# One slot moved in the matrix engine's accumulators: three buffers for a layer's sums, one for the transposes

## The chip, the core and the metric

The kernel runs on one core of a Trainium2 chip. A core has a matrix engine (PE), which writes its sums into a small memory of eight banks, PSUM; a vector engine (DVE) and a scalar engine (ACT), which read PSUM and write SBUF, the working memory; a general engine (POOL); and queues (SP among them) that issue transfers (DMA). Every engine runs its own instructions in order and waits for others by semaphores. The metric is the device time of one execution in microseconds (us), the median of several runs.

## What is computed

The reference runs a recurrence over 768 steps (its result, after a transposition, is x with 3072 tokens of 320 values), then two feed-forward networks. The first is a mixture of experts: each token goes to the expert with the largest logit. The second takes every token.

```python
def _moe_ref(x, modality_id, w_gate, modality_bias, w1, w2):
    logits = x @ w_gate + modality_bias[modality_id]
    e_idx = np.argmax(logits, axis=1)
    ...
    for e in range(E):
        mask = e_idx == e
        ...
        h = np.maximum(x[mask] @ w1[e], 0.0)
        out[mask] = gate_w[mask, None] * (h @ w2[e])

def _moe2_ref(x, w_gate, w_val, w_out):
    g = x @ w_gate
    silu = g * (1.0 / (1.0 + np.exp(-g)))
    val = x @ w_val
    return (silu * val @ w_out).astype(np.float32)
```

Here D is 320, there are 8 experts with 1024 hidden values, and the second network has 1536.

## The kernel before

The recurrence and the routing take the first part of the execution and are not touched. The change lies in `Moe.main`, which does both networks and begins at about 568 us.

*Numbers in two halves.* Each operand of a product is kept as a rounded part and the rest (xh and xl, h and l, hh and hl), and a product is three matmuls into the same sums (`mm3`, L685 to L687). For the last 64 of the 320 input values, both halves share one tile, so there are two matmuls (L695, L696). One *up-projection* (`up`, here called an up) is 8 matmuls: 128 hidden values for all tokens of a group, 384 or 512 columns wide, into one tile `pu`. One *down-projection* (`down`) is 9 or 12 matmuls of 320 columns into the tiles `pd`, one for each 128 tokens, which gather the sums over all hidden values.

*First network.* Tokens sorted by expert come in 8 groups (`sj`), the second of them with 512 tokens, the others with 384. Each group takes 4 passes (`c`), each with two ups; the first group does one up at a time. A pass consists of two ups, their emptying (`evac`: ACT's Relu into hh at L1007, then DVE's hl at L1008), and the two down-projections of the pass before, with splits of the next weights (L745, L746), pieces of the conversion of the second network's weights (`prepare`, which calls L644 to L653) and one token tile of the next group between them. The string `ORD` sets their order. Such a token tile (`xtile`) is three transposes on PE (L729) into one tile `xt`, and its split (`xsplit`): ACT's two copies at L699, then DVE's xl (L700) and x (L701). The first three passes of a group have one each, the fourth has none. Only the second group is made ready in one go: its tile 0 in the last pass of the first group, then, at L1112 to L1117, tiles 1, 2 and 3 with one down-projection behind tile 1.

*A loop for what is left* (L1080 to L1096) stands between, for tokens that eight groups don't hold. With these inputs it runs no times; its branch is a meeting point of all engines.

*Second network.* Tokens come in blocks of 256 or 384, with 12 steps over the hidden values; blocks 0 to 3 do 6 steps each in a first round and 6 in a second one. A step takes two ups (`pg`, `pv`), ACT's Silu of the one (L1192), DVE's product with the other (L1194), ACT's hh (L1197), DVE's hl (L1201) and the down-projections of the step before. Token tiles of the next block (`xt2`, after ACT's product with the gate at L1060) come one in a step, on three following steps. Up to about 850 us the weights are still being converted.

*PSUM.* Three pools share the eight banks, and a tile fills one:

```python
psX=ctx.enter_context(tc.tile_pool(name="psX",bufs=2,space=PS))
psU=ctx.enter_context(tc.tile_pool(name="psU",bufs=2,space=PS))
psD=ctx.enter_context(tc.tile_pool(name="psD",bufs=4,space=PS))
px=lambda: psX.tile([128,3,128],F32,tag="xt",name="xt")
def put(n): return psU.tile([128,WIDE],F32,tag="pu",name="pu")[:,0:n]
```

A pool gives its buffers in turn, and the first write into a buffer waits until everything that read its last tile has ended. The first pool also serves the routing's few products (`rt`), and `put` serves both networks' ups.

Of the kernel before, what the change touches and what calls it, by code (L numbers as in the profile page):

```python
# [15 lines left out]
PS = bass.MemoryType.PSUM  # L16
# [552 lines left out]
SL=384; WIDE=512; NSTAT=8; NMAX=16; NT=SL//128; ROWS=NMAX*SL+WIDE-SL  # L569
# [5 lines left out]
def first(j):  # L575

    return NT*j+((WIDE-SL)//128 if j>1 else 0)
# [110 lines left out]
def up(T,out,w,x,fs,between=None):  # L688


    wh,wl=w; xh,xl,x2=x
    for k in range(2):
        mm3(T,out,wh[:,k,fs],wl[:,k,fs],xh[:,k],xl[:,k],k==0,False)
        if between and k==0: between()
    T.matmul(out,wh[:,2,fs],x2,start=False,stop=False)  # L695
    T.matmul(out,wl[:,2,fs],x2,start=False,stop=True)  # L696
# [5 lines left out]
class Moe:  # L702
# [266 lines left out]
    def main(s, LG, y1, gd, wg, wv, wo, out):  # L969
        tc=s.tc; nc=s.nc; V,A,G,T=nc.vector,nc.scalar,nc.gpsimd,nc.tensor; C=s.C  # L970
        s.gd=gd
        with ExitStack() as ctx:
# [1 line left out]
            s.stp=ctx.enter_context(tc.tile_pool(name="stp",bufs=2))  # L974
            W,between,nbetween=moe2_weights(tc,pool,s.stp,wg,wv,wo)
            P=ctx.enter_context(tc.tile_pool(name="m1",bufs=1)); s.wp.append(P)
            psX=ctx.enter_context(tc.tile_pool(name="psX",bufs=2,space=PS))
            psU=ctx.enter_context(tc.tile_pool(name="psU",bufs=2,space=PS))
            psD=ctx.enter_context(tc.tile_pool(name="psD",bufs=4,space=PS))
            px=lambda: psX.tile([128,3,128],F32,tag="xt",name="xt")  # L980
            def put(n): return psU.tile([128,WIDE],F32,tag="pu",name="pu")[:,0:n]
# [23 lines left out]
            def evac(pu,n):  # L1005
                hh,hl=hht(n)
                A.activation(hh,pu,AF.Relu)  # L1007
                V.scalar_tensor_tensor(hl,pu,0.0,hh.bitcast(F32),ALU.max,ALU.subtract)  # L1008
                return hh,hl
            def down(pd,first,last,hh,hl,wh,wl):  # L1010
                for i in range(len(pd)):
                    ts=slice(128*i,128*i+128)
                    mm3(T,pd[i][:,0:320],hh[:,ts],hl[:,ts],wh,wl,first,last)
            def ystile(): return P.tile([128,WIDE//128,322],F32,tag="ys",name="ys")
            def store(pd,rows,ids,last=False):
                ys=ystile()[:,0:len(pd)]
                V.tensor_copy(ys[:,:,320:322].bitcast(I32),ids)
                for i in range(len(pd)):
                    (V.tensor_copy if i in (0,3) else A.copy)(ys[:,i,0:320],pd[i][:,0:320])
                    if last: nc.sync.dma_start(rows[128*i:128*i+128],ys[:,i])  # L1020
                if not last: nc.sync.dma_start(rows.rearrange("(i p) d -> p i d",p=128),ys)
# [52 lines left out]
            def loop(n):  # L1074

                wx=W["g"]; ws=W["v"]
                f=lambda t: t.bitcast(F32)
                x=(wx[0][:,0:2,512:896],wx[1][:,0:2,512:896],wx[0][:,2,512:896]); h1=tuple(t[:,:,896:1024] for t in wx)
                h2=tuple(t[:,0:1,896:1216] for t in ws); hh=tuple(t[:,2,896:1280] for t in ws)
                with tc.If(n>NSTAT), tc.For_i(NSTAT,n,1) as jr:  # L1080
                    xg=[s.xg() for i in range(NT)]
                    s1=s.stp.tile([128,3,128],F32,tag="cvm",bufs=1,name="s1r"); s2=s.stp.tile([128,1,320],F32,tag="cva",bufs=1,name="s2r")
                    ix=P.tile([128,NT,2],I32,tag="id",bufs=6,name="id")
                    V.tensor_copy(ix[:],R['slot'][:,bass.ds(jr*NT+(first(2)-3*NT),NT)])
                    e=nc.sync.value_load(R['ei'][0:1,bass.ds(jr,1)],min_val=0,max_val=7)
                    for i in range(NT):
                        G.indirect_dma_start(xg[i][:,0:320],None,s.xd,IOA(ap=ix[:,i,0:1],axis=0))
                        s.xtile(x,xg[i],i,px())
                    pd=[px()[:].rearrange("p a b -> p (a b)"),px()[:].rearrange("p a b -> p (a b)"),put(SL)]; pu=put(SL)
                    for c in range(8):  # L1090
                        s.wsplit(s.wload1(s1,e,c),h1); s.wsplit(s.wload2(s2,e,c),h2)
                        up(T,pu,h1,x,slice(0,128))
                        A.activation(hh[0],pu,AF.Relu)
                        V.scalar_tensor_tensor(hh[1],pu,0.0,f(hh[0]),ALU.max,ALU.subtract)
                        down(pd,c==0,c==7,*hh,h2[0][:,0],h2[1][:,0])
                    store(pd,y1[bass.ds(jr*SL+(WIDE-SL),SL),:],ix[:])  # L1096
            def steps(i):
                for q in range(Q['RS'][i] if i<len(Q['RS']) else 4):
                    if crit: (crit.pop(0) or (lambda: (gx(1),next(between))))()
            load1(2); load2(1); steps(0)  # L1100
            for p in range(NP):
# [4 lines left out]
                if sj==0:  # L1106
                    for j in range(2):
                        pu=put(SL); up(T,pu,S1[p],X[0],fs[j],(lambda: steps(1)) if 2*p+j==0 else None); hs=evac(pu,SL)
# [24 lines left out]
                def xt():  # L1133
                    if sj+1<NSTAT and c<3:
                        if c==0: X[sj+1]=s.xalloc(sj+1)
                        s.xtile(X[sj+1],GX[sj+1][c],c,px())
                        if c==2:
                            if sj==1: loop(n)
                            gx(sj+2)
# [147 lines left out]
```

## Time and profile before

| | us |
|---|---|
| median of the runs shown (lowest, highest) | 1197.05 (1196.72, 1200.76) |
| the profiled execution's own time | 1195.36 |
| its span, first to last instruction | 1193.0 |
| PE busy (share of the span) | 1067.8 (90%) |
| DVE busy | 755.1 (63%) |
| ACT busy | 585.9 (49%) |
| POOL busy | 317.9 (27%) |

PE's busy time counts a matmul until its modelled end, and matmuls overlap: one of 384 columns takes 0.34 us in the profile, and the next starts 0.175 after it. The profile gives an engine's idle time with the instruction that ended it, its releaser. Idle time of an engine that others don't wait for costs nothing.

### The profile page before, as it was taken

Reading aid. Unit: us, or ns where it says so; the run is one execution under the profiler, and the core shown is the slowest. Engines: PE = TensorE matmul, PEld = TensorE weight load, DVE = VectorE, ACT = ScalarE, POOL = GpSimd, SP = SyncE. Lnnn points to the kernel's source line nnn. Section 1 sums busy time; section 2 is a strip of 40 time slices with the busy share of each in tenths; the row PEclk is TensorE's granted clock in tenths of the full one; section 3 lists DMA queues with packets and bytes.
Section 4 is the critical chain, followed back from the end, with each engine's and each line's share of the span. In section 5 each row is a group of like instructions: output and inputs, shape, how many; then the busy total and the mean of one; then the engine's idle time right before and its main releaser. Section 6 shows DMA issues by size and latency. Waiting matters only on the chain. (4 is left out here: it accounts for less than half of the span.)

```text
span 1193.0 us, 26716 instructions
## 1 busy us (share of the span) xinstructions
PE 1067.8 (90%) x10413; PEld 1003.7 (84%) x10413; DVE 755.1 (63%) x1666; ACT 585.9 (49%) x1414; POOL 317.9 (27%) x342
## 2 busy tenths in 40 slices
PE   5458789799799788988889999989999999999998
PEld 4448678688688687878779899989999999999998
DVE  4897885965955859673747988878853333333332
ACT  5435556667566456555345565555532233232332
POOL 7634224124222203012344434412000311201100
PEclk9658899889899699999899999999999999999999
DMA  5555257257445353441555667542200100100000
GB/s 97 97 84 98 42 105 121 48 113 150 88 91 97 62 121 68 87 102 44 156 167 169 194 202 227 150 115 79 61 1 12 39 29 17 34 1 29 17 23 12
DMA packets 278326, 102.79 MB, mean 86 GB/s; under 512 B 235344, under 2 KB 272976, under 8 KB 278192
## 3 DMA queue, kind: packets, MB, share of 16 engines
q1 hardware_dynamic: 270880, 86.05, 32.6%
q0 software_dynamic: 3856, 11.02, 3.1%
q10 hardware_dynamic: 3456, 3.93, 1.0%
q8 instruction: 85, 1.39, 0.5%
q14 instruction: 49, 0.40, 0.1%
HBM read 77.56 MB, written 23.40 MB: 85 GB/s over the span
## 5 line engine op out<-in xcount | busy, mean ns | idle before, releaser
L1194 DVE TENSOR_TENSOR s<-s,pu 128x384 f32<-128x384 f32 (+1 forms) x108 | 55.0, 510 | 167.9 <-PE pu L696 158.9
L342 DVE TENSOR_TENSOR tmp<-Lb,Pm 128x126 f32<-128x126 f32 (+45 forms) x248 | 110.3, 445 | 14.3 <-DMA Lb<-LD 6.4
L1197 ACT CAST hh<-s 128x384 fp32r<-128x384 f32 (+1 forms) x108 | 51.6, 478 | 136.3 <-DVE s L1194 136.3
L1192 ACT ACTIVATE s<-pu 128x384 f32<-128x384 f32 (+1 forms) x108 | 49.0, 454 | 102.8 <-PE pu L696 102.8
L344 DVE TENSOR_TENSOR Pm<-Pm,tmp 128x126 f32<-128x126 f32 (+45 forms) x248 | 88.9, 359 | 7.8
L746 POOL TENSOR_TENSOR l<-s,h 128x768 fp32r<-128x768 f32 (+1 forms) x32 | 59.8, 1869 | 124.3 <-ACT h L745 97.3
L685 PE MATMUL pd<-woh,hh 128*128 128x320 f32 x288 | 89.1, 309 | 0.1
L686 PE MATMUL pd<-woh,hl 128*128 128x320 f32 x288 | 89.1, 309 | 0.1
L687 PE MATMUL pd<-wol,hh 128*128 128x320 f32 x288 | 88.9, 309 | 0.0
L1201 DVE TENSOR_TENSOR hl<-s,hh 128x384 fp32r<-128x384 f32 (+1 forms) x108 | 55.5, 514 | 47.6 <-ACT hh L1197 47.4
L279 POOL TENSOR_TENSOR ks<-I,rawk 64x320 f32<-64x320 f32 x48 | 43.6, 908 | 147.8 <-DVE I L276 56.4
L1162 POOL DMA_INDIRECT out_dram<-ys,id x20 | 19.7, 985 | 235.1 <-DVE ys L1159 105.3
L305 PE MATMUL sc<-kbt,atb 128*128 128x128 f32 x384 | 59.6, 309 | 12.8 <-ACT kbt L217 12.5
L305 PEld LDWEIGHTS sc<-kbt,atb 128*128 128x128 f32 x384 | 53.4, 218 | 16.2 <-ACT kbt L217 15.2
L685 PE MATMUL pd<-h,hh 128*128 128x320 f32 x200 | 61.9, 310 | 0.0
L686 PE MATMUL pd<-h,hl 128*128 128x320 f32 x200 | 61.8, 309 | 0.0
L687 PE MATMUL pd<-l,hh 128*128 128x320 f32 x200 | 61.8, 309 | 0.0
L745 ACT CAST h<-s 128x640 fp32r<-128x640 f32 (+1 forms) x64 | 49.3, 782 | 22.2 <-PE pd L686 7.0
L685 PE MATMUL pu<-xh,h 128*128 128x384 f32 (+1 forms) x128 | 47.8, 373 | 13.8 <-DVE hl L1008 7.8
L272 POOL TENSOR_TENSOR atok<-Wt,rawa 128x320 f32<-128x320 f32 x24 | 24.9, 1037 | 130.5 <-ACT Wt L217 66.7
L450 PE MATMUL pq<-rbd,VT 128*128 128x128 f32 x384 | 56.6, 295 | 2.4 <-ACT rbd L217 1.0
L393 PE MATMUL zz<-pbd,MA 128*104 128x128 f32 x384 | 53.2, 289 | 3.5 <-ACT pbd L217 3.5
(375 smaller groups left out, 3330.3 us busy)
## 6 DMA issues: line engine op xcount, KB each, us to landing
s<-in_moe_w_dram SPq DMA_DIRECT2D x32, 320.0 KB, 3.4
s<-in_moe_w_dram SPq DMA_DIRECT2D x32, 256.0 KB, 3.3
Lb<-LD SPq DMA_DIRECT2D x24, 256.0 KB, 3.8
y<-zrow SPq DMA_DIRECT2D x9, 483.0 KB, 4.5
s<-in_moe_w_dram SPq DMA_DIRECT2D x64, 64.0 KB, 3.1
raww<-in_w_dram SPq DMA_DIRECT2D x24, 160.0 KB, 3.4
rawa<-in_a_dram SPq DMA_DIRECT2D x24, 160.0 KB, 3.7
rawk<-in_k_dram SPq DMA_DIRECT2D x24, 160.0 KB, 3.8
```

The source lines that it names most:

```text
L305: T.matmul(ps[:,q].rearrange("p s j -> p (s j)"),ATB[0][:,4*c+q].rearrange("p s j -> p (s j)"),X[i,c][:,q],start=True,stop=True)
L342: V.tensor_tensor(tmp,L[:,:,j+1:32,j].unsqueeze(2).to_broadcast([128,m,k,ni]), Pm[:,:,0:k,j].unsqueeze(3).to_broadcast([128,m,k,ni]),ALU.mult)
L344: return lambda: V.tensor_tensor(Pm[:,:,0:k,j+1:32],Pm[:,:,0:k,j+1:32],tmp,ALU.add)
L393: T.matmul(ps[0:104,h],u['MA'][:,8*i+4*g+h,0:104],pbd[:,4*g+h],start=True,stop=True)
L450: T.matmul(pq[:,q],X['VT',c][:,q],RBD[0][:,q,cc].rearrange("p s t -> p (s t)"),start=True,stop=True)
L685: T.matmul(out,lh,rh,start=first,stop=False)
L686: T.matmul(out,ll,rh,start=False,stop=False)
L687: T.matmul(out,lh,rl,start=False,stop=last)
L746: (E or s.nc.gpsimd).tensor_tensor(hl[1][:],t[:],hl[0][:].bitcast(F32),ALU.subtract)
L1194: V.tensor_tensor(sg,sg,pv,ALU.mult)
L1197: A.copy(hh,sg)
L1201: V.tensor_tensor(hl,sg,hh.bitcast(F32),ALU.subtract)
```

## The change

One buffer goes from the pool of the transposes to that of the ups. In the loop for what is left, one of the three accumulators comes from the other pool for that reason.

```diff
-            psX=ctx.enter_context(tc.tile_pool(name="psX",bufs=2,space=PS))
-            psU=ctx.enter_context(tc.tile_pool(name="psU",bufs=2,space=PS))
+            psX=ctx.enter_context(tc.tile_pool(name="psX",bufs=1,space=PS))
+            psU=ctx.enter_context(tc.tile_pool(name="psU",bufs=3,space=PS))
...
-                    pd=[px()[:].rearrange("p a b -> p (a b)"),px()[:].rearrange("p a b -> p (a b)"),put(SL)]; pu=put(SL)
+                    pd=[px()[:].rearrange("p a b -> p (a b)"),put(SL),put(SL)]; pu=put(SL)
```

No engine's instructions change their order, but what PE waits for does. This is PE's order in a pass of the first network's middle groups: the end of the down-projections, the token tile of the next group and the first up of the next pass. In brackets is the engine (or transfer queue) whose semaphore an instruction waits for.

```order
 L686 MATMUL pd<-h_9640,hl 128x320
 L687 MATMUL pd<-l_9641,hh 128x320
-L729 MATMUL xt<-ident,xg 128x128 [waits DMASW4_49,PE_49]
+L729 MATMUL xt<-ident,xg 128x128 [waits DMASW4_49,DVE_49,PE_49]
 L729 MATMUL xt<-ident,xg 128x128
 L729 MATMUL xt<-ident,xg 64x128
-L685 MATMUL pu<-xh,h_9684 128x384 [waits DVE_49]
+L685 MATMUL pu<-xh,h_9684 128x384
 L686 MATMUL pu<-xh,l_9685 128x384 [waits Pool_49]
 L687 MATMUL pu<-xl,h_9684 128x384
```

The wait for DVE has moved from the up to the transposes ahead of it. And in the second network, in a step with a token tile:

```order
 L687 MATMUL pd<-wol,hh 128x320
-L729 MATMUL xt<-ident,xg 128x128 [waits DMASW0_49,PE_49,Activation_49]
+L729 MATMUL xt<-ident,xg 128x128 [waits DVE_49,DMASW0_49,PE_49,Activation_49]
 L729 MATMUL xt<-ident,xg 128x128
 L729 MATMUL xt<-ident,xg 64x128
-L685 MATMUL pu<-xh,wgh 128x384 [waits Activation_49]
+L685 MATMUL pu<-xh,wgh 128x384
 L686 MATMUL pu<-xh,wgl 128x384
 L687 MATMUL pu<-xl,wgh 128x384
```

Here the up of the gate (wgh) no longer waits for ACT's Silu, and the transposes again wait for DVE.

## Rows read from the trace of the kernel before

**Rows 1.** Busy time by stretch; columns: stretch, length, each engine's busy time, granted clock
```profile
core 0: us, PE busy (x) PEld busy (x) DVE busy (x) ACT busy (x) POOL busy (x), PEclk, DMA share, GB/s
...
640.00:700.00 60.00, 56.09 (x346) 53.79 (x345) 53.88 (x97) 34.27 (x70) 26.21 (x16) 1.00 0.65 194
700.00:776.00 76.00, 73.90 (x462) 72.53 (x461) 64.20 (x106) 45.48 (x93) 33.24 (x22) 1.00 0.64 192
776.00:812.00 36.00, 30.95 (x217) 29.54 (x216) 28.52 (x60) 19.34 (x42) 8.45 (x9) 1.00 0.38 112
...
852.00:1186.00 334.00, 334.00 (x2203) 333.92 (x2202) 123.79 (x259) 103.47 (x233) 40.80 (x42) 1.00 0.06 20
```

**Rows 2.** Waits from 560 us on: waiting instruction, releaser, total us, times, longest
```profile
PE pu L685 <- DVE hl L1008: 7.8, 10, 1.9
...
PE pu L685 <- ACT s L1192: 1.6, 2, 1.4
```

**Rows 3.** Timeline at the second group's tiles: start, us, instruction, idle and releaser
```profile
595.47 0.49 PE L729 MATMUL xt<-ident,xg 128*128 128x128 f32 x3
...
598.35 0.52 PE L729 MATMUL xt<-ident,xg 128*128 128x128 f32 x3 [0.74 <-PE xt L729]
599.33 0.50 PE L685 MATMUL pu<-xh,h 128*128 128x512 f32 x1 [0.46 <-ACT xh L699]
...
595.90 0.28 DVE L701 TENSOR_TENSOR x<-xt,x 64x128 fp32r<-64x128 f32 x1
...
597.97 0.28 DVE L701 TENSOR_TENSOR x<-xt,x 64x128 fp32r<-64x128 f32 x1
...
599.92 0.28 DVE L701 TENSOR_TENSOR x<-xt,x 64x128 fp32r<-64x128 f32 x1
```

**Rows 4.** Timeline of PE in the first group
```profile
579.05 0.44 PE L685 MATMUL pu<-xh,h 128*128 128x384 f32 x1 [1.91 <-DVE hl L1008]
...
581.90 0.49 PE L903 MATMUL rt<-H,O 128*128 128x92 bf16 x8 [0.65 <-ACT H L896]
```

**Rows 5.** Timeline of PE and DVE between 660 and 700 us
```profile
665.05 0.49 PE L729 MATMUL xt<-ident,xg 128*128 128x128 f32 x3
...
666.31 0.44 PE L685 MATMUL pu<-xh,h 128*128 128x384 f32 x1 [0.76 <-DVE hl L1008]
...
699.30 0.44 PE L685 MATMUL pu<-xh,h 128*128 128x384 f32 x1
...
665.38 0.28 DVE L701 TENSOR_TENSOR x<-xt,x 64x128 fp32r<-64x128 f32 x1
...
698.37 0.28 DVE L701 TENSOR_TENSOR x<-xt,x 64x128 fp32r<-64x128 f32 x1
```

**Rows 6.** Timeline of PE and DVE between 700 and 776 us
```profile
710.30 0.49 PE L729 MATMUL xt<-ident,xg 128*128 128x128 f32 x3
710.54 0.42 PE L685 MATMUL pu<-xh,h 128*128 128x384 f32 x1
...
728.37 0.44 PE L685 MATMUL pu<-xh,h 128*128 128x384 f32 x1 [0.52 <-DVE hl L1008]
...
740.74 0.44 PE L685 MATMUL pu<-xh,h 128*128 128x384 f32 x1 [0.42 <-DVE hl L1008]
...
752.76 0.44 PE L685 MATMUL pu<-xh,h 128*128 128x384 f32 x1 [0.39 <-DVE hl L1008]
...
770.79 0.44 PE L685 MATMUL pu<-xh,h 128*128 128x384 f32 x1 [0.77 <-DVE hl L1008]
...
739.81 0.28 DVE L701 TENSOR_TENSOR x<-xt,x 64x128 fp32r<-64x128 f32 x1
```

**Rows 7.** Timeline of ACT and PE in the second network's first steps
```profile
800.38 0.67 ACT L649 CAST wvh<-cva 128x576 fp32r<-128x576 f32 x1 [0.78 <-DVE cva L648]
...
801.39 0.44 PE L685 MATMUL pu<-xh,wgh 128*128 128x384 f32 x1 [1.36 <-ACT s L1192]
```

**Rows 8.** Timeline of PE and DVE at a block's second tile
```profile
844.56 0.51 PE L729 MATMUL xt<-ident,xg 128*128 128x128 f32 x3
...
844.48 0.28 DVE L701 TENSOR_TENSOR x2t<-xt,x2t 64x128 fp32r<-64x128 f32 x1
```

## The prediction, made before the changed kernel ran

> **What bounds the kernel now.** I read the busy time by stretch first [rows 1]. From 852 us on PE has no idle time (334.00 of 334.00), so nothing that the change does to a wait can shorten that part; whatever PE has gained or lost by 852 is there at the end. From 640 to 700 us the vector engine DVE is as full as PE (53.88 and 56.09 of 60): this stretch has two bounds. From 700 to 776 PE is close to full. From 776 to 812 neither is: 30.95 and 28.52 of 36, and the time goes to a chain between engines. Then the waits, for their totals [rows 2]: PE waits 7.8 us in ten places for the DVE instruction that empties a layer's sums (hl, L1008), which is the whole target in the first network, and 1.6 us for the Silu of ScalarE (ACT, s L1192) in the second. Last, the timeline at the places where such a wait ends and where transposes follow each other [rows 3 to 8].
>
> **What the change does to the waits.** No instruction is moved. The k-th up-projection (I call it an up) used to wait for the emptying of number k-2 and now waits for k-3. A group of three transposes, which used to wait for the emptying (xl, x, L700 and L701) of the group before the last, now waits for the last one. I take the places in order of time.
>
> *First layer, 579 us.* The up waited 1.91 us for hl [rows 4]. With three slots it starts that much earlier. But twelve one-hot matmuls and twelve more (rt, L903) follow, and the thirteenth waits for ACT's H whatever PE does; in the trace it starts at 581.90 after a wait of 0.65. The gain is gone there: 0.
>
> *The tiles of the second token group, 595 us.* Four groups of transposes follow each other closely here. Group 3 (counting from 0) starts at 598.35 in the trace [rows 3]: it waited for the split of group 1, which ends at 597.97 + 0.28 = 598.25. With one slot group 1 has to wait for the split of group 0 until 595.90 + 0.28 = 596.18 instead of starting at 595.47; ACT and DVE have other work queued ahead of its split, so that still ends near 598.25. Group 2 now starts at 598.35, where group 3 did. From such a start to the end of the split is 599.92 + 0.28 - 598.35 = 1.85, so group 3 starts at 600.25, 1.90 later than before. The next up needs its first half and follows 0.98 behind the transposes (599.33 - 598.35). So **+1.9 us**, and it stays: PE has no wait for PSUM again until the barrier at the remainder loop, and DVE's last work before that barrier hangs on PE.
>
> *640 to 700 us.* Where transposes stand in front of an up, the gain is small, for DVE does xl, x and then hl without a pause. At 699.30 the up started behind hl. The new rule holds the transposes until x ends at 698.37 + 0.28 = 698.65 [rows 5]. Add 0.05 to react and the 0.24 by which an undisturbed up follows its transposes (710.54 - 710.30) [rows 6]: 698.94 in place of 699.30. PE can be some 0.35 ahead there, however many waits it saved before (0.76 at 666.31 among them), since DVE has no slack to follow. **Lead 0.35.**
>
> *700 to 776 us.* In one pass out of four there are no transposes; there the wait goes entirely. Those are 728.37, 752.76 and 770.79, with 0.52, 0.39 and 0.77 [rows 6]. At 740.74 transposes stand in front: x ends at 739.81 + 0.28 = 740.09, plus 0.05 and 0.24 gives 740.38, again 0.35. In this stretch DVE has idle time and mostly waits for work that PE releases, so it follows and the leads add: 0.35 + 0.52 + 0.35 + 0.39 + 0.77 = 2.4. The 0.52 can be cut back at those transposes, which without it started 0.27 before x had ended. I take **2.0**.
>
> *776 to 812 us.* The up at 801.39 waited 1.36 for ACT's s, and ACT reached s only after a weight conversion that waited for DVE's [rows 7]. These conversions go back and forth between DVE and ACT for the whole stretch and do not wait for PE. A free slot lets PE run ahead, but the next transposes meet a DVE that is no earlier than its own lead. So 0, and the lead of 2.0 is carried.
>
> *818 and 844 us.* The second transposes of a block start at 844.56 in the trace, and the split before them ends at 844.48 + 0.28 = 844.76 [rows 8]; one block earlier, at 818.36, it is the same 0.2. With one slot they have to wait for it: 0.2 + 0.05 each time, **0.5 off** the lead. From 852 on PE has no wait [rows 1], and no transposes come close to each other: nothing more.
>
> **Sum.** 1.9 - (2.0 - 0.5) = +0.4 us. The profiled execution took 1195.36 us, so it would become 1195.8. The median of the three runs shown is 1197.05, 1.7 above the profiled one; the same difference gives **1197.4 us**. Half a per cent, about what a measurement of this kernel can tell from no change, is 6.0 us.
>
> What the trace of before cannot show is a DVE that runs at other times against GpSimd. The bounds of the lead are 0 (DVE never follows) and 2.4 (all adds up), so the sum lies between 1.9 + 0.5 = +2.4 and 1.9 - 2.4 + 0.5 = 0; I take +0.4 because DVE idles in the stretch where most of the lead arises (64.20 of 76 busy [rows 1]). Around that I allow 2 us each way for shifted overlaps.
>
> **Rivals.**
> *All waits for slots go (faster).* If DVE kept up everywhere, the first network would save the waits after 579, 7.8 - 1.9 = 5.9, and the second the 1.6 for s [rows 2]; only the 1.9 of the second token group is paid. 1.9 - 7.5 = -5.6: 1191.4 us. For it: the waits are real and repeat. The Trainium skill (Perfetto Trace Analysis, Optimization Strategy) says that the same gap coming back on the engine that should be saturated can mean that there isn't enough PSUM for the next tile. By that rule the ten waits are a matter of slots, and the time would be this rival's. The trace agrees where DVE has idle time, from 700 on, and not before. Against it: DVE is 90% busy from 640 to 700 [rows 1], so those waits are DVE's pace and only show up at the slot. Chance 0.1.
>
> *The single transposes slot decides throughout (slower).* Besides the second token group, seven groups of transposes start in the trace before the split ahead of them has ended, from 665.05, which comes 0.61 before x ends at 665.38 + 0.28 [rows 5], to 844.56 with its 0.2 [rows 8]. Together the seven lack 2.9, and 0.05 to react each time makes 3.25. If PE gains nothing (DVE's own work, not the slot, sets each start) and these waits are paid in full, the sum is 1.9 + 3.25 = +5.1: 1202.2 us. It decides from the point where x of the last group ends later than PE arrives; with a PE that runs ahead this happens more often than in the trace. Against it: at 666.31 and 740.74 PE waits right behind the transposes anyhow [rows 5, 6], so those waits only change places. Chance 0.17.
>
> *The change moves no wait at all.* The rows of the instruction order show the wait for DVE gone from the ups and new at the transposes, so only the case remains that the data wait of the next down-projection (hl itself) replaces the slot's. Then the leads are nil: +2.4, inside the first case's bounds. Chance 0.05, 1199.5 us.
>
> **Numbers.** The forecast has 0.68: -2 to +3 around 1197.05, that is 1195 to 1200. To leave out no more than 2 in 10 the range has to reach into both rivals and hold the spread of the runs shown, so 1192.5 to 1201.5. Faster by over 0.5% (below 1191.1) is the far half of the first rival: 0.05. Slower by over 0.5% (above 1203.0) needs the second rival and more: 0.04. Within: 0.91.
>
> **What would show it.** Right: in the waits, PE pu for hl falls from 7.8 to under 3, a new row PE xt for x L701 of 3 to 6 us appears, and the ups at the second token group start about 1.9 later; PE reaches the second network about as it did. Wrong: the row for x L701 is missing or under 1 us (first rival), or over 8 (second), or the stretch 640 to 700 becomes shorter by more than 1 us, which would mean that DVE was not its bound.

## The result and the profile after

The change makes the kernel slower. Its median is 1207.20 us of 8 runs, beside 1199.86 of 8 runs of the kernel before in the same series: a ratio of 1.0062, with a 95% interval of 1.0041 to 1.0084. A second series gave 1.0055 (1.0035 to 1.0076). I had forecast +0.4 us, within a range of 1192.5 to 1201.5; it is +7, and the median lies above the range. The profiled execution took 1202.66 us, its span 1200.5.

Busy time by stretch, columns as in [rows 1], at the same places of the program:

```profile
643.20:704.60 61.40, 55.16 (x346) 53.58 (x345) 55.60 (x97) 34.52 (x70) 28.00 (x18) 1.00 0.64 191
704.60:783.50 78.90, 74.89 (x462) 73.81 (x461) 64.76 (x104) 44.69 (x92) 31.56 (x21) 0.98 0.63 184
...
859.50:1193.50 334.00, 334.00 (x2203) 333.92 (x2202) 123.36 (x259) 103.16 (x232) 41.24 (x42) 1.00 0.06 20
```

The stretch of 60.00 us has become 61.40 and the one of 76.00 has become 78.90. The end is unchanged. In the second row the granted clock is 0.98, where it was 1.00.

The waits from 560 to 860 us, which answer to [rows 2]:

```profile
PE xt L729 <- issue: 8.7, 6, 2.7
...
PE xt L729 <- DVE x L701: 2.4, 2, 1.5
...
PE pu L685 <- DVE hl L1008: 1.2, 2, 1.0
```

The ups' wait for hl fell from 7.8 to 1.2 as forecast. The transposes now wait 2.4 for the last tile's split by name, and 8.7 that the profile puts down to issue. In the timeline these six end 0.10 after such a split too, and so do two more waits, 1.4 in sum, that the profile puts down to the down-projection ahead. That makes 12.5 us. Here are three of them, at the second token group; the rows answer to [rows 3]:

```profile
595.61 0.28 DVE L701 TENSOR_TENSOR x<-xt,x 64x128 fp32r<-64x128 f32 x1
596.00 0.52 PE L729 MATMUL xt<-ident,xg 128*128 128x128 f32 x3 [0.66 <-PE pd L687]
...
597.66 0.28 DVE L701 TENSOR_TENSOR x<-xt,x 64x128 fp32r<-64x128 f32 x1
598.05 0.52 PE L729 MATMUL xt<-ident,xg 128*128 128x128 f32 x3 [0.21 <-issue]
...
599.60 0.28 DVE L701 TENSOR_TENSOR x<-xt,x 64x128 fp32r<-64x128 f32 x1
599.98 0.52 PE L729 MATMUL xt<-ident,xg 128*128 128x128 f32 x3 [1.42 <-issue]
600.97 0.50 PE L685 MATMUL pu<-xh,h 128*128 128x512 f32 x1 [0.46 <-ACT xh L699]
```

The clock is what I had left out. Three stretches of 3.40 us ran at 1.2 GHz (the 0.50 below), where before had 1.00 from 574 to 1191 us:

```profile
579.90:583.30 3.40, 3.05 (x29) 2.85 (x27) 3.30 (x6) 2.87 (x5) 0.00 (x0) 0.50 0.02 5
624.30:627.70 3.40, 3.40 (x9) 2.67 (x8) 0.00 (x0) 0.56 (x1) 1.67 (x2) 0.50 0.95 299
747.20:750.60 3.40, 3.40 (x13) 3.40 (x12) 2.76 (x4) 0.47 (x1) 0.00 (x0) 0.51 0.94 287
```

In the second of them matmuls of 512 columns start 0.43 us apart (624.76, 625.19); ones of the same size before started 0.23 apart (625.43, 625.66).

**Where the time went.** I count every up from the first one of the networks (568.53 us before, 567.65 after), because the recurrence ahead, which is not touched, ended anywhere from 567 to 578 us in the traces of this study. The lateness of the same up against before, with a second trace of the changed kernel in brackets:

| up, time before | lateness, us | forecast by then |
|---|---|---|
| 584.04, behind the one-hot matmuls | 0.80 (0.83) | 0 |
| 599.33, second token group | 2.52 (2.84) | 1.9 |
| 629.41, behind the barrier | 4.09 (4.42) | 1.9 |
| 693.18 | 3.84 (4.15) | 1.55 |
| 699.30 | 5.47 (5.79) | 1.55 |
| 734.26 | 4.49 (4.85) | 1.4 |
| 746.65 | 8.05 (8.42) | 1.1 |
| 776.35, second network | 8.38 (8.78) | -0.1 |
| end | 8.36 (8.91) | 0.4 |

The two traces agree within 0.6 us in every line, and the dips of the clock stand 12, 57 and 180 us from the first up in both. So this is the program, not chance. Of the 8.0 us by which the end exceeds the forecast, the stretch up to 629 us makes 2.2, that from there to 699 1.7 and that from 699 to 776 4.6; the second network takes back 0.5. There are three jumps to explain: at 584 to 629, at 699 and at 734 to 747 us.

The two jumps in the middle begin at DVE. This is before, at 697 us:

```profile
697.12 0.83 ACT L745 CAST h<-s 128x768 fp32r<-128x768 f32 x1 [0.26 <-DMA s<-in_moe_w_dram]
697.85 0.17 DVE L945 TENSOR_TENSOR krank<-scr 128x20 int32<-128x20 f32 x1
698.03 1.84 POOL L746 TENSOR_TENSOR l<-s,h 128x768 fp32r<-128x768 f32 x1 [2.84 <-ACT h L745]
...
737.83 0.83 ACT L745 CAST h<-s 128x768 fp32r<-128x768 f32 x1
738.70 0.76 DVE L653 SCALAR_TENSOR_TENSOR wvl<-cvm,cva 128x576 fp32r<-128x576 f32 x1
738.74 2.42 POOL L746 TENSOR_TENSOR l<-s,h 128x768 fp32r<-128x768 f32 x1 [2.09 <-ACT h L745]
```

and the same instructions after:

```profile
699.69 0.83 ACT L745 CAST h<-s 128x768 fp32r<-128x768 f32 x1
700.60 2.24 POOL L746 TENSOR_TENSOR l<-s,h 128x768 fp32r<-128x768 f32 x1 [2.18 <-ACT h L745]
701.08 1.80 DVE L945 TENSOR_TENSOR krank<-scr 128x20 int32<-128x20 f32 x1
...
741.56 0.84 ACT L745 CAST h<-s 128x768 fp32r<-128x768 f32 x1
742.48 2.40 POOL L746 TENSOR_TENSOR l<-s,h 128x768 fp32r<-128x768 f32 x1 [1.31 <-ACT h L745]
743.23 2.27 DVE L653 SCALAR_TENSOR_TENSOR wvl<-cvm,cva 128x576 fp32r<-128x576 f32 x1
746.23 0.52 PE L729 MATMUL xt<-ident,xg 128*128 128x128 f32 x3 [2.66 <-issue]
```

Before, DVE's instruction was 0.18 and 0.04 us ahead of POOL's l, and took 0.17 and 0.76. After, POOL was first, and DVE's took 1.80 and 2.27: it ended behind POOL's. At the second place the split behind it came late, the transposes waited 2.66 for the single buffer, and the clock dipped from 747.20 on.

### The profile page after: what moved, and what is told of

The parts are those of the page before. It is cut to its first block, busy times and chain, and to the rows that moved or that the text cites. A ratio compares the mean times of both kernels' runs of the same rounds, so it can differ in the third digit from the quotient of the medians.

```text
span 1200.5 us, 26743 instructions
## 1 busy us (share of the span) xinstructions
PE 1068.5 (89%) x10413; PEld 1006.4 (84%) x10413; DVE 758.4 (63%) x1666; ACT 586.1 (49%) x1414; POOL 319.0 (27%) x342
## 5 line engine op out<-in xcount | busy, mean ns | idle before, releaser
L746 POOL TENSOR_TENSOR l<-s,h 128x768 fp32r<-128x768 f32 (+1 forms) x32 | 60.2, 1882 | 133.6 <-ACT h L745 106.3
L746 DVE TENSOR_TENSOR l<-s,h 128x640 fp32r<-128x640 f32 (+1 forms) x32 | 42.9, 1341 | 20.7 <-ACT h L745 20.5
```

The source lines that it names most:

```text
L746: (E or s.nc.gpsimd).tensor_tensor(hl[1][:],t[:],hl[0][:].bitcast(F32),ALU.subtract)
```

## The experiments

Theory A: PE's waits at the single transposes buffer make the loss. Theory B: DVE meets POOL's l (L746) at worse times. Theory C: the clock's dips. A fourth, D, came up on the way. For the slots I gave out four single banks by a rule for each of three stages (up to the second token group's tiles; the rest of the first network; the second network):

```diff
-            psX=ctx.enter_context(tc.tile_pool(name="psX",bufs=1,space=PS))
-            psU=ctx.enter_context(tc.tile_pool(name="psU",bufs=3,space=PS))
+            psS=ctx.enter_context(tc.tile_pool(name="psS",bufs=1,space=PS))
+            sl=Slots(psS,('ring', 'ring', 'ring'))
...
+    SEQ={"two":((0,1),(2,3)),"one":((0,),(1,2,3)),"least":((0,),(1,2)),"ring":((0,1,2,3),(0,1,2,3))}
+        i=next(b for b in s.old if b in s.SEQ[s.r][kind])
```

In each pair of SEQ stand the banks for transposes and those for ups; the one unused longest is taken.

All results; the last four columns are lengths in us in the one trace of each kernel: from the first up of the networks to the first of the second token group, the middle (641.76 to 776.35 us in before), the whole to the end, and the dips' distance from the first up.

| kernel | median, runs | before beside it | ratio, 95% interval | to 2nd group | middle | whole | dips |
|---|---|---|---|---|---|---|---|
| before | | | | 30.8 | 134.6 | 624.5 | none |
| before, again | 1200.45, 1 | 1203.55 | | 30.4 | 135.5 | 625.0 | 226 |
| changed | 1207.20, 8 | 1199.86 | 1.0062 [1.0041, 1.0084] | 33.3 | 138.9 | 632.8 | 12, 57, 180 |
| changed, again | 1205.68, 7 | 1199.06 | 1.0055 [1.0035, 1.0076] | 33.6 | 138.9 | 633.4 | 12, 57, 180 |
| ring | 1202.34, 12 | 1202.79 | 0.9995 [0.9975, 1.0016] | 31.2 | 135.7 | 626.2 | 13 |
| start two and two | 1204.29, 12 | 1202.79 | 1.0021 [1.0005, 1.0037] | 31.5 | 139.0 | 629.4 | 11, 175 |
| middle two and two | 1206.97, 12 | 1202.79 | 1.0035 [1.0018, 1.0051] | 34.5 | 136.2 | 633.8 | 15, 35, 59 |
| loss alone | 1203.16, 12 | 1202.79 | 1.0013 [0.9993, 1.0032] | 32.6 | 136.8 | 629.7 | 33 |
| loss alone, filled | 1198.67, 12 | 1199.06 | 0.9999 [0.9983, 1.0014] | 32.7 | 136.2 | 626.9 | none |
| hold | 1204.56, 12 | 1203.55 | 1.0014 [0.9994, 1.0035] | 33.7 | 134.8 | 629.4 | 13, 34 |
| before, no l | 1187.86, 6 | 1201.23 | 0.9884 [0.9849, 0.9920] | 29.5 | 127.1 | 614.6 | none |
| changed, no l | 1190.00, 6 | 1201.23 | 0.9900 [0.9866, 0.9934] | 32.6 | 125.5 | 619.0 | 12, 33 |
| before, l in pieces | 1198.80, 12 | 1201.23 | 0.9983 [0.9963, 1.0003] | 30.8 | 137.4 | 626.6 | 119, 228 |
| changed, l in pieces | 1203.19, 12 | 1201.23 | 1.0022 [1.0002, 1.0042] | 33.6 | 135.7 | 630.1 | 12, 33 |
| ring, l in pieces | 1201.00, 12 | 1203.55 | 0.9986 [0.9962, 1.0009] | 32.0 | 136.2 | 629.5 | 12, 57, 176 |
| late split | 1201.60, 12 | 1199.06 | 1.0019 [1.0002, 1.0036] | 31.1 | 138.9 | 629.9 | 231 |
| mid split | 1201.16, 12 | 1199.06 | 1.0017 [0.9997, 1.0037] | 30.7 | 140.0 | 631.5 | 177, 232 |

Two things limit what the table can say. First, the kernels from the ring on all use this new form of the slots, and each does better against before by its time than by its one trace. The loss alone, for one, is 1.6 us slower by its ratio, and its trace is 5.2 longer than that of before. The gap is 2.3 to 6.7 us in all thirteen, and 0.9 and 2.3 in the changed kernel. No run has the slots of before or of the change in the new form and nothing else, so the reason is not shown; I compare the stages by the traces. Second, at the meeting point of L1080, ahead of the middle, PE waits 1.9 to 2.0 us in ten traces, both of before among them, but 0.81 in six (start, the loss alone, its filled form, and with two and two buffers the ones without l, in pieces and with the late split) and 1.54 with the mid split. This step of 1.2 is part of the whole lengths, and why it comes stays open.

### Which stage loses

Ring: `('ring','ring','ring')`.

> The four banks of the transposes and the ups are given out as one ring of four, whoever asks next. Then neither waits for the split just ahead: PE's row for x L701 and its row for hl L1008 both fall to under 1 us. Theory A (the waits at the single transposes slot make the loss, and DVE falls behind because PE holds it up): nothing is lost at the second token group, and the time is that of before or below, by 1 to 5 us. Theory B (what costs is that DVE's and POOL's instructions meet at other times, whichever slot moved): PE runs ahead as in the changed kernel, DVE's long instructions come in other places, and the time is 2 to 6 us above before, though no wait for a slot is left. Theory C (the clock's dips behind PE's waits of 2 us and more): no dip at 624 and 747 us, 2.5 us less than the changed kernel, 4 to 5 above before.

Start: `('two','one','one')`.

> Two and two buffers up to the second token group's tiles, the changed rule (one and three) from there on. Theory A: the 1.8 us at the second group's tiles come back, and with them the dip of the clock at 624 us with its 1.2, so the time is 3 us below the changed kernel, about 4 above before. Theory B: from 640 us on everything runs 2 to 3 us earlier against POOL, and what DVE meets there is drawn anew: between 6 us below and 3 above the changed kernel. If the shift of the start is taken back later because DVE sets the pace of 640 to 700 us, the time is that of the changed kernel within 1 us.

Middle: `('one','two','one')`.

> The changed rule (one and three) up to the second token group's tiles and in the second network, two and two in the first network's seven middle groups. Theory A: the loss of the middle groups goes, 4 us; what is left is the second group's 1.8, the dip behind it and 0.5 of the second network: 2 to 4 us above before. PE's row for hl L1008 is back at 5 to 6 us. Theory B: the middle runs as in before but 2 to 3 us later, so DVE's long instructions come in yet other places: 2 to 8 us above before.

Loss alone: `('least','least','least')`.

> One buffer for the transposes and two for the ups; a bank stays unused. Only the loss of the change, without its gain. Theory A, with the third buffer for the ups worth little since DVE follows at its own pace: within 2 us of the changed kernel. If the third buffer is worth the lead of 2 us that I forecast: 2 us above the changed kernel, 9 above before. Should the third buffer itself do harm (PE runs ahead into places where it then waits longer): below the changed kernel by 2 us or more.

By its time the ring loses nothing that can be measured, as A had it; its trace is 1.7 us longer than that of before. Yet it has the jump at 738 us too (DVE's L653 takes 2.26), which speaks for B. What follows differs: from 734 to 776 us the ring loses 0.8, the changed kernel 3.9 and the start kernel, with the same slots there, 4.0. In the ring no transposes wait behind the late split, and the clock doesn't dip. By their ratios start and middle are 2.5 and 4.2 us above before, in or beside the ranges of both theories, and decide nothing. Undoing the start leaves the middle at 139.0, as in the changed kernel; undoing the middle makes it 136.2. The surprise is the loss alone: with two buffers for the ups instead of three the middle is shorter, 136.8 against 138.9. So the third buffer itself does harm there, and A, which makes the single one guilty, can't be the whole. L653 shows where: with whole l it takes 2.26 or 2.27 in all four traces in which the ups have more than two buffers in this stretch (the changed kernel twice, ring, start), and 0.76 in the five in which they have two and the split stands where before has it.

### POOL's l taken away, and cut

No l: up weights from the third pass on without their low half.

```diff
-                if p<NP: S1[p]=s.wsplit(L1.pop(p),s.h1tiles(p),V if p in Q['V1'] else None)
+                if p<NP: t=L1.pop(p); h=s.wp[0].tile([128,3,256],F32R,tag="h1",bufs=2,name="h1"); A.copy(h[:],t[:]); S1[p]=(h,s.once("Z",lambda: (lambda z: (G.memset(z[:].bitcast(F32),0.0),z)[1])(s.wp[0].tile([128,3,256],F32R,tag="l1",bufs=2,name="l1"))))
```

> The slots of before (two and two). Left out: POOL's low halves of the first network's up weights from the third pass on; a tile of zeros stands in their place, so POOL has no l (L746) in this stretch and ACT, DVE and PE keep their instructions. In the traces so far a DVE instruction that works from SBUF to SBUF ends only when POOL's l ends (0.81 becomes 1.95, 0.31 becomes 1.97). Theory B: these long ones are gone, DVE gets back some 15 us between 640 and 776 us, PE is then the bound, and the main part is 4 to 8 us shorter than in before. If POOL's l is not what holds DVE, the long instructions stay and the time is that of before within 2 us.

> The same with the slots of the change (one for the transposes, three for the ups); the same low halves are left out. Theory B (the change loses in the middle groups because DVE meets POOL's l in worse places): without POOL's l what is left is the second token group's 1.8 and a lead of 1 to 2.5, so this kernel is within 2 us of its two-and-two twin, most likely 0 to 1 above, and no jump stands at 687 to 699 and 734 to 746 us. Theory A (PE's waits at the single slot hold up PE and DVE): 4 to 8 us above the twin. Theory C (the clock): the difference is a whole number of dips of 3.4 us at half clock, 1.4 us each.

The middle by busy time, columns as in [rows 1]: of before, of the changed kernel, of before without l, and of the changed one without l.

```profile
641.76:776.35 134.59, 128.58 (x797) 124.92 (x795) 116.74 (x198) 79.26 (x161) 58.11 (x38) 1.00 0.64 193
```

```profile
644.98:783.85 138.87, 128.62 (x797) 125.95 (x794) 119.00 (x195) 78.97 (x161) 58.24 (x38) 0.99 0.63 187
```

```profile
637.75:764.85 127.10, 126.25 (x797) 124.82 (x794) 100.58 (x198) 81.31 (x162) 14.54 (x15) 1.00 0.68 203
```

```profile
649.95:775.46 125.51, 125.28 (x796) 124.77 (x794) 100.07 (x197) 80.89 (x162) 14.51 (x15) 1.00 0.70 206
```

B's point holds. DVE's 198 instructions of before take 100.58 here; with POOL's l they take 116.74 of 134.59. And without l the change gains 1.6 us in the middle (127.10 to 125.51), close to the 2.0 that I had forecast for it; with l it costs 4.3 (134.59 to 138.87). Neither kernel has a jump at 699 or 746 us. Over the whole program the twin with the changed slots is 4.4 longer in the trace (2.1 by the medians), because of the start: 3.1 up to the second group, 1.4 with its dip at 33 us and 1.2 at L1080. That was more than the 0 to 2 that I expected there.

Pieces: POOL's l in three instructions.

```diff
-        (E or s.nc.gpsimd).tensor_tensor(hl[1][:],t[:],hl[0][:].bitcast(F32),ALU.subtract)
+        for q in ([slice(k,k+1) for k in range(3)] if E is None and t.shape[1]==3 else [slice(0,t.shape[1])]): (E or s.nc.gpsimd).tensor_tensor(hl[1][:,q],t[:,q],hl[0][:,q].bitcast(F32),ALU.subtract)
```

> The slots of before; POOL's l of 768 columns in three pieces of 256. Theory B: DVE waits for the end of the piece that is running, 0.65 us at most instead of 1.85, unless it is caught by each piece in turn; then the long instructions shrink from 1.95 to 1.1 to 1.4, DVE gets back 5 to 10 us between 640 and 776, and the main part is 2 to 5 us shorter than in before. If DVE stays locked until POOL's third piece ends: no change, or up to 2 us longer for POOL's added instructions.

> The slots of the change; POOL's l in three pieces. Theory B: nearer to its twin than the 7 us between the two kernels: 0 to 3 us above. Theory A: 5 to 8 us above the twin.

Both missed. DVE got nothing back: it is busy 120.05 us of the first one's middle (116.74 before), and that middle is 137.4, not shorter. The second stands 4.4 us above its twin by the medians, between the ranges of the two theories. Between the twins the third buffer again gains in the middle: 137.4 to 135.7, of which a dip at 119 us in the first explains part. Against before the pieces bring less than 0.4%, and the interval includes none.

### The split at another time

```diff
-'ORD': '1dD2bBx'
+'ORD': 'dD2bBx1'
```

(The mid split is `'dD2bB1x'`.)

> The slots of before; the split of the weights for the pass after next (ACT's h, POOL's l) is issued at the end of a pass, behind the token tile, no longer at its start behind the two emptyings. POOL's l then runs beside DVE's xl, x and hl, which read PSUM and in no trace so far were held by POOL. Theory B: most of DVE's long instructions between 640 and 776 us go, DVE gets back 8 to 14 us, some of it lost because ACT's emptying comes 0.83 later behind h: the main part 2 to 7 us shorter than in before. If POOL meets other instructions of DVE instead: within 2 us of before.

> The same with the split issued just ahead of the token tile, so that ACT's h stands ahead of the tile's copies, which come 0.83 later, and POOL's l begins with DVE's last instruction of the pass. Theory B: 1 to 6 us below before; which of the two is better depends on whether ACT has room ahead of the copies or behind them.

Both missed. DVE got its time back in the late split (108.55 busy in the middle, 116.74 before), and the middle is still 4.3 us longer, for PE now waits for POOL's l itself; no such row stands among the waits of before in that stretch:

```profile
PE pu L686 <- POOL l L746: 4.6, 11, 0.7
```

### The clock

```diff
-s.xtile(X[1],GX[1][i],i,px())
+wm=sl.bank(3,"warm")[:,0:SL]; [T.matmul(wm,S1[p+1][0][:,0,fs[0]],X[0][0][:,0],start=True,stop=True) for q in range((0,4,2,8)[i])]; s.xtile(X[1],GX[1][i],i,px())
```

> One transposes buffer, two for the ups, as in the kernel that measures the loss alone; added are 4, 2 and 8 matmuls of 384 columns into the unused bank ahead of the second token group's tiles 1, 2 and 3, where PE waits for the split anyway. Their sums are read by nobody. Theory C (the dip of 3.4 us at half clock between 32 and 60 us, seen in all five traces with one transposes buffer there and in none of five without, follows those waits): no dip there, and the ups of the second group run 1.4 us earlier than in that kernel; the tiles themselves come no later. If the dip comes from something else, it stays, and the time is the same.

The loss alone, then the same with PE's waits filled, each in 3.40 us that begin some 33 us from the first up:

```profile
611.00:614.40 3.40, 3.40 (x9) 2.48 (x8) 0.53 (x2) 0.13 (x1) 0.00 (x0) 0.50 0.29 104
```

```profile
600.00:603.40 3.40, 3.26 (x14) 2.48 (x15) 1.04 (x3) 0.84 (x3) 0.00 (x0) 1.00 0.48 172
```

As C had it: no dip, and the second group's first up as late as without filling (32.7 and 32.6 from the first up), since the transposes still wait for the split. At 604.85 us of before the one kernel is 3.20 late and the other 1.85; the dip cost 1.4. So the dip at 33 us hangs on those waits. For the one at 57 us, which the changed kernel has, this isn't shown: it begins 0.5 us behind PE's wait of 1.98 at L1080, and the ring with pieces, which has no single buffer, dips there as well. Before waits the same 1.98 there without a dip. What stands is a count: all seven traces with one buffer for the early transposes and no filling have a dip between 33 and 59 us, of the ten others one.

### The changed kernel and before once more, and the lead taken away in two passes

> The changed kernel once more, for a second trace and for times beside the other experiments. What belongs to the kernel comes back, what belongs to one execution does not: the second token group 1.8 late, a dip of the clock behind it between 32 and 60 us from the start of the networks, the jumps of 2 to 4 us at 687 to 699 and 734 to 746 us. If all of them come back, the difference of 5 to 7 us is a matter of fixed meetings between DVE and POOL; if the jumps are elsewhere or gone, it is chance. Time: 5 to 7 us above before.

> The kernel before once more, for a second trace. In the first one a transfer held ACT's h for 0.26 us at 697 us, POOL's l began behind DVE's L945, and that took 0.17; in every other trace with POOL's l in one piece the same pass cost 1.65 more. If that was chance, this trace has L945 at 1.8 and the ups from 699 us on 1.65 later than the first, and no dip of the clock between 32 and 60 us from the start of the networks. If it belongs to the slots of before, L945 takes 0.17 again.

The changed kernel's jumps all came back. In before's second trace L945 took 0.17 again, and the transfer held ACT's h the same 0.26:

```profile
701.48 0.84 ACT L745 CAST h<-s 128x768 fp32r<-128x768 f32 x1 [0.26 <-DMA s<-in_moe_w_dram]
...
702.21 0.17 DVE L945 TENSOR_TENSOR krank<-scr 128x20 int32<-128x20 f32 x1
```

So it was not luck of one trace. It isn't the middle's slots either: with two and two there and the changed start, nothing held h and L945 was caught:

```profile
709.12 0.83 ACT L745 CAST h<-s 128x768 fp32r<-128x768 f32 x1
...
710.02 1.97 POOL L746 TENSOR_TENSOR l<-s,h 128x768 fp32r<-128x768 f32 x1 [2.47 <-ACT h L745]
710.21 1.82 DVE L945 TENSOR_TENSOR krank<-scr 128x20 int32<-128x20 f32 x1
```

The loss alone and its filled form, 2.0 and 0.7 late at that place, lose the same 1.65 there. So does the start kernel, which is 0.7 early there, so a late start isn't the reason either; and the ring, where POOL's l holds L652 (2.39) in place of L945. Why the transfer is in time in all of them stays open.

Hold: the rule of the change, but in two passes an up takes the bank of the up before the last.

```diff
+            sl=Slots(psS,('one', 'one', 'one', 'one-hold'))
...
+        l=[b for b in s.old if b in s.SEQ[s.r.split("-")[0]][kind]]; i=l[1 if kind and s.r.endswith("-hold") else 0]
...
-                fs=[slice(128*j,128*j+128) for j in range(2)]
+                fs=[slice(128*j,128*j+128) for j in range(2)]; sl.stage(3 if p in (24,25) else min(sj,1))
```

> The changed kernel, but in two passes of the first network (those whose ups start at 728 and 734 us in the trace of before) an up takes the bank of the up before the last, as with two buffers; everything else has the third buffer as before. Theory D (the third buffer does harm there: the lead of 0.8 that it gives brings POOL's l ahead of DVE's wvl at L653, which is then held 1.5, PE's next transposes wait 2.8 for the single buffer, and the clock dips): the lead of 1.0 by 734 goes, DVE's wvl takes 0.76 again, no dip at 747, and the ups behind it are 1 to 3 us earlier than in the changed kernel by 753 us, with less room for PE. If the loss has another cause: the lead goes and the loss stays, 1 us later than the changed kernel.

Its timeline at the place of the jump:

```profile
747.98 0.83 ACT L745 CAST h<-s 128x768 fp32r<-128x768 f32 x1
...
748.86 0.76 DVE L653 SCALAR_TENSOR_TENSOR wvl<-cvm,cva 128x576 fp32r<-128x576 f32 x1
748.89 2.44 POOL L746 TENSOR_TENSOR l<-s,h 128x768 fp32r<-128x768 f32 x1 [2.08 <-ACT h L745]
...
750.35 0.52 PE L729 MATMUL xt<-ident,xg 128*128 128x128 f32 x3 [0.22 <-PE pd L687]
```

D holds in each part. DVE's wvl is 0.03 ahead of POOL and takes 0.76; the transposes wait 0.22, not 2.66; the clock stays at 1.00; the up at 752.76 of before is 4.87 late, not 7.48. The lead of 1.0 by 734 us is gone (5.71 late instead of 4.49), and the middle is 134.8 us, 4.1 shorter than in the changed kernel and as long as in before. Less freedom for PE, in two passes of 32, made the trace shorter. The times point the same way (0.14% above before, where the changed kernel had 0.62% and 0.55%), but the hold kernel has the new form of the slots, which does better by its times.

> A version that may beat both: the ring of four with POOL's l in three pieces. The ring alone was level with before, the pieces alone 2 us better. If the two add, 2 to 4 us below before; if the ring's lead is eaten by meetings with POOL again, level with before.

Whether the two add isn't shown: the ring with pieces has a ratio of 0.9986, the pieces alone 0.9983. No version that computes everything beats before by more than its interval.

## Why the prediction was wrong, step by step

*What bounds the kernel* was right: nothing is gained or lost from 852 us on (8.36 late at 853.59 and at the end).

*First layer, 579 us: 0.* The first up's gain is gone at the one-hot matmuls, as forecast; but PE, early, waited 2.28 and 0.35 for H where it had waited 0.65 [rows 4], and the clock fell at 579.90. That made it 0.80 late. All eight traces with more than two banks for the early ups have a dip 12 to 15 us from the first up; of the nine others one has, at 11. In sum PE waited about as long before (1.91 and 0.65 [rows 4]) without a dip, so why it comes isn't shown. I had put the clock at nothing, without a reason.

*Second token group: +1.9.* Right: 1.7 and 2.0 in the two traces (2.52 - 0.80, 2.84 - 0.83), with tiles at 596.00, 598.05 and 599.98 as the rule for one slot gives them; they start 0.10 after the split, where I had added 0.05. What I left out is the dip at 57 us, 1.6 us: the pass from 622.13 to 629.41 took 7.27 before and 8.84 after. Its cause stays open, for it follows the wait at L1080, which before has too.

*640 to 700 us: lead 0.35.* Right where it was measured alone: 4.09 late at 629.41, 3.84 at 693.18, a lead of 0.25. DVE is the bound there. Then 1.65 is lost at L945, which I had not reckoned with; why POOL came first there stays open.

*700 to 776 us: lead 2.0.* This is the step that failed, and the largest miss. "DVE has idle time and mostly waits for work that PE releases, so it follows and the leads add." By 734 us the lead was there: 0.98, even more than I had by then. But ACT and POOL follow PE's lead too, and DVE, whose own instructions had no lead, did not follow (from the first up, DVE's wvl starts 5.4 us later than before, ACT's h 4.6): ACT's h came 0.8 earlier against DVE, so that POOL's l got ahead of wvl (L653). That cost 1.5 at DVE, PE's 2.66 at the single slot and a dip: 3.6 us by 746.65. The hold kernel shows this; the kernels without l show that the lead is worth 1.6 where POOL doesn't stand in the way. My allowance for "a DVE that runs at other times against GpSimd" was 2 us each way; L945 and L653 alone take 1.65 and 1.5, both the same way.

*776 us on: 0, then 0.5.* Right in size: from 776.35 to the end the two traces of before take 416.7 and 416.6 us, seven with the changed rule there 416.6 to 417.7.

*The second rival* (slower, 1202.2) came nearest, and its sign appeared: rows for the transposes' wait above 8 in sum. Its mechanism alone did not decide in the middle: the hold kernel and the loss alone keep the single slot and lose nothing from 734 to 746 us. But it is part of it: the ring, caught at the same L653 without the single slot, loses 0.8 by 776 us where the changed kernel loses 3.9. The rule that I weighed, of the Trainium skill (Perfetto Trace Analysis, Optimization Strategy), that a gap coming back can mean too little PSUM, would have given a gain; with POOL's l in its way the third buffer gave none.

*The sum.* 0.8 + 1.7 + 1.6 for the start, -0.25 + 1.65 up to 699, -1.0 + 3.6 + 0.3 from there to 776, 0 behind it: 8.4, as measured. Of this I had 1.9 and the leads.

## What to carry to other kernels

A buffer that lets one engine run ahead moves every engine that follows it; before counting the gain, look at which pairs of instructions on the others stand within the size of the lead of each other, and price a change of their order by the longest such instruction in the trace. Price a new wait of PE with the clock behind it, not by its length alone. And a stall that shows up at a slot is worth its length only if the engine behind it can follow.

## What the runs showed of the hardware

*DVE and POOL.* DVE instructions from SBUF to SBUF that met POOL's l ended only behind it, L945 0.04 us and wvl 0.61: wvl's 0.76 became 2.27, L945's 0.17 became 1.80, even for 20 columns. The one that comes second pays: before, with wvl first, POOL's l took 2.42 instead of 1.84; after, it took 2.40, for DVE's L652 was running when it began, and wvl then waited for it. DVE's xl and hl, which read PSUM, kept their 0.42 and 0.56 beside a running l. The Trainium skill states it (SBUF — State Buffer, SBUF: two separate sides): DVE and GpSimd share a pair of ports, and whichever starts first has it for its whole instruction, against a DVE instruction with two inputs in SBUF or in a two-port mode. The trace agrees in these pairs, but not in one: before, at 754.67, DVE's L645 with one input started 0.07 us ahead of POOL's l and took 2.27 instead of 0.39, ending 0.32 behind it. In sum, l holds some 16 us of DVE's time in the middle (116.74 busy with l, 100.58 without). I had not used it.

*The clock.* In the changed kernel it fell to 1.2 GHz for 3.40 us at three places, the same in two executions: behind a wait of 2.28 us for ACT's H, behind one of 1.98 at L1080 and behind one of 2.66 at the single slot. The first two cost 0.8 and 1.6 us, the one at 33 us in the loss alone 1.4. Before has waits of 1.91 and of 1.98 at the first two places and no dip, so the length of one wait doesn't tell whether the clock falls. The Trainium skill (TensorE: Matmul & The Clock Gate, A second HAM failure mode: psum-queue depth-cycling) tells of a kernel in which PE idles briefly between groups of matmuls, at its PSUM banks, so often that the clock swings. Here the dips at 33 us (the loss alone) and at 180 us stand behind waits for a PSUM bank too, but behind few and longer ones, the longest of 1.42 and 2.66 us; those at 12 and 57 us stand behind other waits. So the trace agrees in part.
